# Filler products by an estimated fill, 64-column score products, slack ahead of attention steps, and chunks 8 to 15 in one stretch

## The chip, the cores and the metric

The kernel runs on one core of one Trainium2 chip. The metric is the device time of one execution in microseconds (us), as the median of several runs. The engines are named as in the profile: PE (TensorE, matmuls; PEld is its weight load), DVE (VectorE), ACT (ScalarE), POOL (GpSimd) and SP (SyncE, which issues most DMAs). A line such as L741 is a line of the kernel's file before the change.

## The reference

Eight batches of eight heads, 576 tokens, 64 features a head. For each head two attentions are added: one over q, k and v averaged over groups of four tokens (144 by 144 scores), whose output is repeated four times, and one in a band, where a token sees tokens at a distance under 4. Then the 4608 tokens, 512 features each, go through `h = x @ w_in` (512 to 2048), `g = h * cos(h)` and `g @ w_out` (2048 to 512).

```
scores = where(|i - j| < 4, scale * q @ k.T, -1e9);  out_local = softmax(scores) @ v
out_up = repeat(softmax(scale * mean4(q) @ mean4(k).T) @ mean4(v), 4)
x = (out_up + out_local) laid out as tokens x 512
h = x @ w_in;  out = (h * cos(h)) @ w_out
```

## The kernel before

The FFN works on 12 tiles of 384 tokens and on 16 chunks of 128 of the 2048 hidden features. One **step** is one chunk of one tile: the first product (gemm1, L741, 12 matmuls of 384 columns into a `ph` bank, of which there are two), the activation on ACT and DVE (tr, gh, gl; the DVE operations on tr are L753 and L756, and L756 is the last reader of the `ph` bank), and two steps later on PE the second product (gemm2, L777, 9 matmuls of 512 columns into three `po` banks). Numbers are split into a high and a low part of a shorter format, hence x3h and x3l, gh and gl, wi and wo with two halves. There are 192 steps, counted here from 0; `PASSES` gives their order. The tiles 0, 1 and 2 take turns by four chunks (steps 0 to 47), so that a chunk's weights are needed late; then each tile runs through all 16 chunks (tile 3 is steps 48 to 63, tile 4 steps 64 to 79, and so on). At the end of a pass the `po` banks are copied out (ob, L793) and stored, or added to the output in memory by a DMA that POOL issues (L802). Weights come as 64-bit words and are split on ACT, DVE and POOL (`w_load`, `w_split`, L420 to L431, L399).

The attention works on 32 **units**, a batch and a pair of heads each; a unit has five parts. `u_qk` loads q and k and sums groups of four (qkd, L490); both have one buffer for the batches from 2 on. `u_v` does the same for v. `u_s` computes both scores (from batch 2 on L539, the band, and L555, the averaged tokens), the maxima, the exps and the sums; `u_t` normalizes and transposes (L650) and, from batch 2 on, moves the band's weights by DMA (ptb); `u_pv` multiplies by v (L667 and L686; L679 for the batches 0 and 1) and writes x, from `xd` and `xs` (L698) to x#h (L713) and x#l (L399). The four x tiles form a ring: x3h is the high part of an x tile in place 3. The batches 0 and 1 lie ahead of the steps or between the first ones, with other shapes (L546, L679) and with buffers cut out of weight chunks not loaded yet.

Nothing of the order is written by hand. Every part gives its operations to `Plan.op` with an engine, an estimated duration and its buffers; each has a due time in steps (`at`, `unit`). `Plan.schedule` simulates the engines with priorities and keeps the best of eight rounds; the instructions are then recorded on each engine in the order of the planned starts, and each engine runs its own in order. While recording, wherever PE has a planned hole ahead of 300 us, **wide products** of the identity with itself (L916, 128 by 512, nobody reads them) are put into a free bank for 0.8 of the hole.

## Time and profile before

| what | us |
|---|---|
| median of 3 runs (lowest, highest) | 1006.36 (1006.16, 1006.46) |
| the profiled execution | 1007.08 |
| its span, first to last instruction | 1005.3 |
| PE busy / DVE / ACT / POOL in the span | 985.1 / 678.2 / 610.2 / 223.8 |
| first product of step 0 begins | 52.64 |
| first product of step 4 begins; steps follow without filler from here | 107.18 |
| first product of step 48 begins | 309.84 |

The page gives one profiled execution. Busy time is the time in which an engine computes; an engine that waits for a semaphore, or only issues DMAs, is idle. The granted clock is the share of TensorE's full clock that it was given. A row of the timeline is a group of equal instructions that follow each other: start, time from the first's start to the last's end, what it writes and reads, shapes, count, and in brackets the idle time of the engine ahead of it and what ended it. Matmuls overlap, so the pace of a group is read from its start to the start of the next. A matmul of 32-bit numbers shows as two records.

### The profile page before, as it was taken

The page shows a single profiled execution, that of the slowest core. Times are in us where ns is not written, and L with a number is a line of the kernel's source. Part 1 is how long each engine was busy: PE and PEld are TensorE (multiplying, and loading weights), DVE is VectorE, ACT ScalarE, POOL GpSimd, SP SyncE. Part 2 cuts the span into 40 slices and gives each one's busy share as a digit, 9 for nine tenths or more (in the row PEclk, how much of TensorE's full clock was granted, in tenths as well). Part 3 has the DMA queues.
Part 4 walks back from the last instruction along what each step waited for, and adds up shares of the span by engine and source line. Part 5 has one row for each costly group of instructions (what it writes and reads, how often), then busy time and mean ns, then how long its engine had stood idle before and what let it go on. Part 6 is the DMA issues. An engine that isn't in the chain of part 4 may idle for free.

```text
span 1005.3 us, 23882 instructions
## 1 busy us (share of the span) xinstructions
PE 985.1 (98%) x9932; PEld 850.3 (85%) x9932; DVE 678.2 (67%) x1362; ACT 610.2 (61%) x1174; POOL 223.8 (22%) x280
## 2 busy tenths in 40 slices
PE   8898999999998999999999999999999999999998
PEld 5556898899886888889888888888888888899997
DVE  7699999985686678464758957655657765433433
ACT  4357688876665656555547746654646665655554
POOL 6685334631242203000002211200001300000000
PEclk9699999999999999999999999999999999999999
DMA  7874733332453422210212412201112320100000
GB/s 230 250 249 159 255 119 62 72 59 45 75 131 105 84 66 70 66 33 28 82 48 71 127 49 58 82 26 36 64 52 73 116 60 4 37 1 1 32 1 32
DMA packets 41051, 80.70 MB, mean 80 GB/s; under 512 B 4976, under 2 KB 16240, under 8 KB 40944
## 3 DMA queue, kind: packets, MB, share of 16 engines
q1 hardware_dynamic: 37056, 72.11, 23.2%
q0 software_dynamic: 3888, 7.08, 5.0%
q8 instruction: 78, 1.28, 0.5%
q14 instruction: 29, 0.24, 0.1%
HBM read 57.93 MB, written 16.52 MB: 74 GB/s over the span
## 4 chain that ended last, share of the span: by engine, by line
PE 89%; DVE 5%; DMA 1%; issue 1%; ACT 1%; POOL 1%; SPq 0%; ACTq 0%; POOLq 0%; DVEq 0%
PE bank L777 38%; PE bank L741 38%; PE bank L539 2%; PE bank L916 2%; PE bank L686 2%; PE bank L555 2%; PE bank L667 2%; PE bank L650 1%; DMA q<-qT 1%; PE bank L679 1%; DVE su L610 1%; DVE xxh L421 0%; DVE tr L756 0%; PE bank L546 0%; DVE xxh L425 0%
## 5 line engine op out<-in xcount | busy, mean ns | idle before, releaser
L777 PE MATMUL bank<-wo,gh 128*128 128x512 f32 x1152 | 363.9, 397 | 0.0
L777 PEld LDWEIGHTS bank<-wo,gh 128*128 128x128 f32 x1152 | 210.2, 188 | 38.1 <-issue 3.2
L777 PE MATMUL bank<-wo,gl 128*128 128x512 f32 x576 | 227.7, 396 | 0.0
L752 ACT ACTIVATE tr<-bank,bmagic 128x384 f32<-128x384 f32 x192 | 110.9, 578 | 114.1 <-PE bank L741 109.2
L756 DVE SCALAR_TENSOR_TENSOR tr<-tr,bank 128x384 f32<-128x384 f32 x192 | 105.0, 547 | 108.1 <-ACT tr L751 107.4
L753 DVE SCALAR_TENSOR_TENSOR tr<-tr,bank 128x384 f32<-128x384 f32 x192 | 105.7, 551 | 82.8 <-ACT tr L752 81.8
L750 ACT ACTIVATE tr<-tr 128x384 f32<-128x384 f32 x192 | 100.6, 524 | 77.0 <-DVE tr L753 76.4
L758 ACT ACTIVATE gh<-tr 128x384 fp32r<-128x384 f32 x163 | 85.3, 523 | 91.9 <-DVE tr L756 90.1
L399 DVE TENSOR_TENSOR gl<-tr,gh 128x384 fp32r<-128x384 f32 x154 | 91.7, 596 | 63.5 <-ACT gh L758 59.8
L777 PEld LDWEIGHTS bank<-wo,gl 128*128 128x128 f32 x576 | 108.1, 188 | 23.5
L741 PE MATMUL bank<-x3h,wi 128*128 128x384 f32 x384 | 106.9, 338 | 1.6 <-DVE tr L756 1.0
L741 PE MATMUL bank<-x0h,wi 128*128 128x384 f32 x384 | 107.0, 339 | 0.0
L741 PE MATMUL bank<-x1h,wi 128*128 128x384 f32 x384 | 107.0, 339 | 0.0
L741 PE MATMUL bank<-x2h,wi 128*128 128x384 f32 x384 | 106.8, 339 | 0.0
L751 ACT ACTIVATE tr<-tr 128x384 f32<-128x384 f32 x192 | 100.9, 525 | 6.1
L399 POOL TENSOR_TENSOR gl<-tr,gh 128x384 fp32r<-128x384 f32 x38 | 43.3, 1139 | 268.2 <-DVE gh L759 174.7
L741 PEld LDWEIGHTS bank<-x3h,wi 128*128 128x128 f32 x384 | 70.2, 188 | 4.3 <-DVE tr L756 1.5
L741 PEld LDWEIGHTS bank<-x0h,wi 128*128 128x128 f32 x384 | 70.2, 188 | 2.4 <-DVE wxo L569 0.2
L741 PEld LDWEIGHTS bank<-x1h,wi 128*128 128x128 f32 x384 | 70.2, 188 | 2.4 <-issue 0.4
L741 PEld LDWEIGHTS bank<-x2h,wi 128*128 128x128 f32 x384 | 70.2, 188 | 2.2 <-DVE xxh L425 0.2
L741 PE MATMUL bank<-x3l,wi 128*128 128x384 f32 x192 | 64.6, 336 | 0.1
L741 PE MATMUL bank<-x0l,wi 128*128 128x384 f32 x192 | 64.5, 336 | 0.0
(199 smaller groups left out, 1457.2 us busy)
## 6 DMA issues: line engine op xcount, KB each, us to landing
vl<-vl SPq DMA_DIRECT2D x26, 384.0 KB
out<-ob SPq DMA_DIRECT2D x36, 256.0 KB
wdi<-w_in SPq DMA_DIRECT2D x16, 512.0 KB
wdo<-w_out SPq DMA_DIRECT2D x16, 512.0 KB
q<-qT SPq DMA_DIRECT2D x26, 292.0 KB
k<-kT SPq DMA_DIRECT2D x26, 292.0 KB
vd<-vdn SPq DMA_DIRECT2D x26, 288.0 KB
out<-ob POOLq DMA_DIRECT2D x27, 256.0 KB, 5.3
```

What stands on the lines that cost most here:

```text
L399: f = lambda e: lambda: e.tensor_tensor(out=out(), in0=in0(), in1=in1(), op=ALU.subtract)
L539: pe.matmul(banks[h].get()[BS * g:BS * (g + 1), c:c + BS], q.get()[hs, o:o + BS], k.get()[hs, o:o + BS], start=True, stop=True)
L555: pe.matmul(banks[h].get()[:HD, i * SD:(i + 1) * SD], qkd.get()[hs, 0, i * HD:(i + 1) * HD], qkd.get()[hs, 1, :], start=True, stop=True)
L667: pe.matmul(banks[0].get()[64 * h:64 * h + 64, 2 * SD:3 * SD], vd.get()[:, kh, 64 * h:64 * h + 64], ptd.get()[:, h, kh, :], start=(kh == 0 ...
L741: pe.matmul(ph.get()[:, :m], w[:, i, kc, :], x[:, kc, :], start=(n == 0), stop=(n == 3 * KC - 1))
L750: act.activation(tr.get(), tr.get(), AF.Sin, scale=PI)
L751: return act.activation(tr.get(), tr.get(), AF.Square)
L752: pl.op("ACT", _act(m, True, 1), lambda: act.activation(tr.get(), h(), AF.Identity, bias=bmagic), r=[ph], w=[tr])
L753: pl.op("DVE", _dve(m), lambda: dve.scalar_tensor_tensor(out=tr.get(), in0=tr.get(), scalar=MAGIC, in1=h(), op0=ALU.subtract, op1=ALU.subt ...
L756: pl.op("DVE", _dve(m), lambda: dve.scalar_tensor_tensor(out=tr.get(), in0=tr.get(), scalar=0.5, in1=h(), op0=ALU.subtract, op1=ALU.mult), ...
L758: pl.op("ACT", _act(m, False), lambda: act.activation(gh.get(), tr.get(), AF.Copy), r=[tr], w=[gh], alts=[("DVE", _dve(m / 2), lambda: dve ...
L777: pe.matmul(o, (gh, gh, gl)[k].get()[:, sl], wo.get()[:, (0, 1, 0)[k]], start=(c == c0 and k == 0), stop=(c == c1 - 1 and k == 2))
```

## The change

Three things change, and some with them. (1) While recording, the planner keeps a list of when PE was in use and how far each group fills the array (`util`, its own estimate by shape); ahead of each PE operation planned in its first 115 us, it puts in wide products until its estimated share reaches 0.55. (2) From batch 2 on the band's scores are 24 matmuls of 64 columns instead of 48 of 32: k is loaded into `kz`, which has two planes, one for each head, with zeros in the other head's 64 rows, so that one matmul over all 128 rows gives both heads side by side. Its sums over four tokens are now two DVE instructions, without POOL as the other choice; `ptd` shares its place with `smd`; the band's mask gets 16-bit numbers; in planning, an operation of PE that belongs to these attention parts is assumed ready 0.5 us after an operation of another engine that it needs (`SLACK`); a unit's parts are due 1.1 steps apart instead of 1.4 and units at least 2.25 steps apart instead of 1.5. (3) For tiles 0 to 2, chunks 8 to 15 are one pass instead of two. The core of the diff:

```diff
-PASSES = [(t, c, c + NF) for c in range(0, NC, NF) for t in range(3)] + [(t, 0, NC) for t in range(3, NT)]
+PASSES = [(t, c, e) for c, e in ((0, NF), (NF, 2 * NF), (2 * NF, NC)) for t in range(3)] + [(t, 0, NC) for t in range(3, NT)]
...
+SLACK = 0.5
...
-           fgap=0.4, f0=0.8, fend=300.0, warm=0, fill=0.8)
+           fgap=0.4, f0=0.8, fend=300.0, warm=0, fill=0.8, share=0.55, watch=115.0)
...
+        o.slack = SLACK if eng == "PE" and self.name in ("u_s", "u_t", "u_pv") and self.arg[0] >= NEARLY else 0.0
...
-                    o.preds.append((d, d.lat))
-                    d.succs.append((o, d.lat))
+                    g = d.lat + (0.0 if "PE" in d.alts else o.slack)
+                    o.preds.append((d, g))
+                    d.succs.append((o, g))
...
-    band = const.tile([P, NSEG, BS], F32, name="band")
+    band = const.tile([P, NSEG + 2, BS], BF16, name="band")
+    kz = const.tile([P, 2, SP_], F32, name="kz")
...
-        return sb({"ptl": "sml", "xs": "vd4"}.get(name, name), 2 if name == "ptl" else n, shape)
+        return sb({"ptl": "sml", "xs": "vd4", "ptd": "smd"}.get(name, name), 2 if name == "ptl" else n, shape)
...
+        def load():
+            for hs, h in halves:
+                ins = sp.dma_start(kz[hs, h], kT[b, pr][hs])
+            return ins
+
+        def sums():
+            for hs, h in halves:
+                dve.tensor_reduce(out=qkd.get()[hs, 1], in_=kz[hs, h, PAD:PAD + S].rearrange("p (a r) -> p a r", r=4), axis=AX.X, op=ALU.add)
...
-                for f in range(2):
-                    for n in range(NSEG):
-                        for g in range(4):
-                            h = (g // 2 + f) % 2
-                            hs, o, c = slice(64 * h, 64 * h + 64), (4 * n + g) * BQ, LQ + BS * n
-                            pe.matmul(banks[h].get()[BS * g:BS * (g + 1), c:c + BS],
-                                      q.get()[hs, o:o + BS], k.get()[hs, o:o + BS], start=True, stop=True)
+                for n in range(NSEG):
+                    for g in range(4):
+                        o, c = (4 * n + g) * BQ, LQ + 2 * BS * (n % 3)
+                        pe.matmul(banks[n // 3].get()[BS * g:BS * (g + 1), c:c + 2 * BS].rearrange("p (h n) -> p h n", h=2),
+                                  q.get()[:, o:o + BS], k.get()[:, :, o:o + BS], start=True, stop=True)
...
-            last = max(lo - 2.5 + (hi - lo - 1.0) * i / (NPAIR - 1), last + 1.5)
-            unit(last, 1.4, 2.5, b, i)
+            last = max(lo - 2.5 + (hi - lo - 1.0) * i / (NPAIR - 1), last + 2.25)
+            unit(last, 1.1, 2.5, b, i)
...
+    def wide(s):
+        return pe.matmul(s[2].get(), ident_b, ident_b.unsqueeze(1).broadcast_to([P, 4, P]), start=True, stop=True)
+
+    def share(o, t):
+        e = t + o.dur
+        return (sum(max(0.0, min(y, e) - max(x, e - 3.41)) * u for x, y, u in spent[-60:]) + o.dur * o.util) / 3.41
...
+                    while 4.0 < o.start < CFG["watch"] and share(o, max(cur, o.start)) < CFG["share"]:
+                        wide(s)
+                        spent.append((cur, cur + 0.22, 1.0))
+                        cur += 0.22
```

The planned order then comes out different on every engine. Three places follow, before and changed; in the changed file L563 is the band's scores, L579 the averaged ones, L691 and L710 the value products, L765 and L801 gemm1 and gemm2, L722 the sum that gives xs, L425 to L431 and L403 the weight split and its last part, L924 the wide products.

The first place is on DVE, where the last unit of batch 0 gives its x and chunk 0's weights are split, ahead of step 0. Before:

```order
L698 TENSOR_TENSOR wxo_481<-bank,wxo_396 128x3x96 x2
L423 TENSOR_SCALAR xxh<-xxh 128x512 x2
L425 SCALAR_TENSOR_TENSOR xxh<-wdi_391,xxh 128x512
L425 SCALAR_TENSOR_TENSOR xxh<-wdo_455,xxh 128x512
L698 TENSOR_TENSOR wxi_567<-bank,wxi_559 128x3x96
L427 SCALAR_TENSOR_TENSOR xxh<-wdi_391,xxh 128x512
L427 SCALAR_TENSOR_TENSOR xxh<-wdo_455,xxh 128x512
L698 TENSOR_TENSOR wxi_567<-bank,wxi_559 128x3x96
L399 TENSOR_TENSOR wi_932<-xxh,wi_932 128x512
L399 TENSOR_TENSOR wo_937<-xxh,wo_937 128x512
L399 TENSOR_TENSOR x0l<-wxi_567,x0h 128x384
```

Now:

```order
L722 TENSOR_TENSOR wxo_480<-bank,wxo_396 128x3x96 x2
L658 STREAM_TRANSPOSE wxi_555<-wxi_555 128x384
L429 SCALAR_TENSOR_TENSOR xxh<-wdi_391,xxh 128x512
L427 TENSOR_SCALAR xxh<-xxh 128x512
L431 SCALAR_TENSOR_TENSOR xxh<-wdi_391,xxh 128x512
L429 SCALAR_TENSOR_TENSOR xxh<-wdo_455,xxh 128x512
L722 TENSOR_TENSOR wxi_571<-bank,wxi_555 128x3x96 x2
L431 SCALAR_TENSOR_TENSOR xxh<-wdo_455,xxh 128x512
L403 TENSOR_TENSOR x0l<-wxi_571,x0h 128x384
L403 TENSOR_TENSOR x1l<-wxi_571,x1h 128x192
L403 TENSOR_TENSOR wo_967<-xxh,wo_967 128x512
```

The split of chunk 0 has moved ahead of the last unit's sums (L698 on bank and wxi), and x0l follows those sums almost at once.

The second place is on PE, the start of the unbroken steps (x1h is the x of step 4; the wide products ahead of these rows are left out). Before:

```order
L539 MATMUL bank<-k,q 32x32 x48
L555 MATMUL bank<-qkd 72x144 x4
L741 MATMUL bank<-x1h,wi_932 128x384
L741 MATMUL bank<-x1l,wi_932 128x384
```

Now the scores of the first unit of batch 2 stand behind gemm2 of step 17 and ahead of gemm1 of step 20:

```order
L801 MATMUL bank<-wo_2018,gh 128x512 x2
L801 MATMUL bank<-wo_2018,gl 128x512
L563 MATMUL bank<-kz,q 32x64 x24
L579 MATMUL bank<-qkd 72x144 x4
L765 MATMUL bank<-x2h,wi_1892 128x384
```

They have left the front of the stream and gone into it; wide products fill the place.

The third place is on PE in front of step 64, the first of tile 4, whose x (x0h, x0l) the value products finish. Before:

```order
L667 MATMUL bank<-ptd,vd 64x144 x4
L686 MATMUL bank<-ptb,vl 64x48 x24
L741 MATMUL bank<-x3h,wi_3176 128x384
...
L777 MATMUL bank<-wo_3090,gh 128x512 x2
L777 MATMUL bank<-wo_3090,gl 128x512
L741 MATMUL bank<-x0h,wi_932 128x384
```

Now:

```order
L691 MATMUL bank<-smd,vd 64x144 x4
L710 MATMUL bank<-ptb,vl 64x48 x24
L563 MATMUL bank<-kz,q 32x64 x24
L579 MATMUL bank<-qkd 72x144 x4
L765 MATMUL bank<-x0h,wi_949 128x384
```

Between the value products and the first product that reads their x there was a whole step; now there are only the next unit's scores.

## Rows read from the trace of the kernel before

**Rows 1.** The page: busy time, share and instructions of each engine over the span, then PE's busy share and granted clock in 40 slices of the span, in tenths.

```profile
PE 985.1 (98%) x9932; PEld 850.3 (85%) x9932; DVE 678.2 (67%) x1362; ACT 610.2 (61%) x1174; POOL 223.8 (22%) x280
...
PEclk9699999999999999999999999999999999999999
```

**Rows 2.** The table of stretches: from:to and length in us, busy time and instruction count of each engine in it, granted clock, share of the DMA engines and GB/s.

```profile
23.00:33.00 10.00, 8.96 (x122) 5.62 (x121) 7.53 (x19) 6.19 (x25) 4.63 (x6) 0.50 0.82 249
...
40.00:50.00 10.00, 9.47 (x165) 6.20 (x165) 4.74 (x8) 2.79 (x7) 7.21 (x13) 0.50 0.79 240
50.00:107.00 57.00, 51.06 (x1021) 34.58 (x1019) 55.93 (x109) 37.58 (x97) 38.23 (x42) 1.00 0.64 205
107.00:300.00 193.00, 193.00 (x1517) 172.39 (x1513) 160.04 (x302) 144.07 (x269) 74.64 (x77) 1.00 0.43 98
300.00:321.00 21.00, 17.25 (x220) 13.29 (x220) 13.34 (x31) 10.44 (x18) 6.84 (x10) 0.92 0.45 120
321.00:860.00 539.00, 538.63 (x5462) 474.90 (x5461) 356.67 (x748) 322.96 (x584) 71.58 (x89) 1.00 0.21 61
860.00:1000.00 140.00, 140.00 (x702) 126.49 (x701) 57.33 (x103) 73.98 (x138) 0.00 (x0) 1.00 0.03 12
```

**Rows 3.** The chain of work that ended last, near its end: start, us, what.

```profile
988.56 2.10 PE bank L741 x12
990.66 2.08 PE bank L777 x9
992.75 2.10 PE bank L741 x12
```

**Rows 4.** DVE's timeline ahead of step 0, the three rows with a wait for PE or for a copy behind it (start, us, engine, line, operation, out<-in, shapes, count, idle before).

```profile
30.51 0.31 DVE L466 TENSOR_SCALAR wxi<-bank 128x144 f32<-128x144 f32 x1 [0.85 <-PE bank L667]
...
37.93 0.82 DVE L698 TENSOR_TENSOR wxo<-bank,wxo 128x288 f32<-128x288 f32 x2 [0.86 <-ACT wxo L465]
...
46.65 0.46 DVE L698 TENSOR_TENSOR wxi<-bank,wxi 128x288 f32<-128x288 f32 x1 [5.26 <-ACT wxi L465]
```

**Rows 5.** PE's timeline in the same time.

```profile
25.09 1.05 PE L679 MATMUL bank<-wxi,wxo 32*64 32x24 f32 x28
27.19 2.12 PE L679 MATMUL bank<-wxi,wxo 32*64 32x24 f32 x68 [1.04 <-issue]
...
35.16 0.88 PE L667 MATMUL bank<-wxi 72*64 72x144 f32 x8
35.98 1.59 PE L679 MATMUL bank<-wxo,wxi 32*64 32x24 f32 x96
...
40.13 0.87 PE L546 MATMUL bank<-k,q 64*32 64x32 f32 x48 [1.63 <-issue]
...
41.55 2.33 PE L679 MATMUL bank<-wxi,wxo 32*64 32x24 f32 x76
44.28 0.84 PE L679 MATMUL bank<-wxi,wxo 32*64 32x24 f32 x20 [0.40 <-issue]
45.05 1.23 PE L667 MATMUL bank<-wxo 72*64 72x144 f32 x8
```

**Rows 6.** PE's timeline: 14 wide products at the full clock, and the scores ahead of step 4.

```profile
57.70 3.20 PE L916 MATMUL bank<-ident_b 128*128 128x512 bf16 x14 [0.23 <-ACT smd L597]
...
104.47 0.79 PE L539 MATMUL bank<-k,q 64*32 64x32 f32 x63
```

**Rows 7.** PE's timeline in the steady stretch: a block of scores, a block of value products, eight transposes, each with the row behind it.

```profile
436.05 1.02 PE L539 MATMUL bank<-k,q 64*32 64x32 f32 x96
437.00 0.71 PE L555 MATMUL bank<-qkd 64*72 64x144 f32 x8
...
451.61 0.91 PE L686 MATMUL bank<-ptb,vl 64*64 64x48 f32 x48
452.45 0.50 PE L777 MATMUL bank<-wo,gh 128*128 128x512 f32 x1
...
330.12 0.67 PE L650 MATMUL bank<-ident,smd 72*72 72x72 f32 x8
330.58 0.71 PE L777 MATMUL bank<-wo,gh 128*128 128x512 f32 x2
```

**Rows 8.** PE's timeline around step 48.

```profile
300.39 0.71 PE L667 MATMUL bank<-ptd,vd 72*64 72x144 f32 x8
...
309.84 0.44 PE L741 MATMUL bank<-x3h,wi 128*128 128x384 f32 x1 [1.05 <-DVE tr L756]
...
312.25 0.45 PE L741 MATMUL bank<-x3h,wi 128*128 128x384 f32 x1 [0.56 <-ACT x3h L713]
...
314.24 0.67 PE L650 MATMUL bank<-ident,smd 72*72 72x72 f32 x8 [0.78 <-DVE smd L616]
...
316.33 1.33 PE L539 MATMUL bank<-k,q 64*32 64x32 f32 x92 [0.50 <-ACT ptd L465]
...
320.76 0.33 PE L741 MATMUL bank<-x3h,wi 128*128 128x384 f32 x1
```

**Rows 9.** DVE's timeline ahead of step 48, and the piece of the chain of work in the same time.

```profile
307.05 0.75 DVE L490 TENSOR_REDUCE qkd<-q 128x144 f32<-128x576 f32 x1 [5.31 <-DMA q<-qT]
...
300.30 6.73 DMA q<-qT
```

**Rows 10.** Timelines: value products and the x that follows from them (PE, DVE), the last split of a weight chunk (POOL), the first product of step 39 (PE).

```profile
393.86 0.44 PE L741 MATMUL bank<-x3h,wi 128*128 128x384 f32 x1
...
396.24 0.35 DVE L399 TENSOR_TENSOR x0l<-vd,x0h 128x192 fp32r<-128x192 f32 x1
...
228.07 1.29 POOL L399 TENSOR_TENSOR wo<-xxh,wo 128x512 fp32r<-128x512 f32 x1 [4.89 <-ACT wo L431]
...
258.35 0.33 PE L741 MATMUL bank<-x0h,wi 128*128 128x384 f32 x1
```

**Rows 11.** Groups of instructions by line: count, busy us, mean ns of one, idle before.

```profile
L490 DVE TENSOR_REDUCE qkd<-k 128x144 f32<-128x576 f32 x19 | 14.2, 745 | 1.5 <-DMA k<-kT 1.4
```

More of the change, by code (lines that the diff above doesn't have):

```diff
@@ L75 @@
     __slots__ = ("eng", "dur", "fn", "tab", "deps", "sdeps", "now", "start", "end", "lat", "name", "arg", "preds", "succs",
-                 "i", "fin", "bank", "alts", "boost", "shares")
+                 "i", "fin", "bank", "alts", "boost", "shares", "util", "slack")
 class Plan:
@@ L447, in ub @@
         shape, n, chunk, off = UNIT[name]
+        if name == "k" and (b >= NEARLY or not pr):
+            return pl.buf(lambda: kz if b >= NEARLY else kz[:, 0], "k.0")
         if b == 1 and pr and name in "qk":
@@ L474, in u_qk, with zero @@
         bk = bank(b, "t") if early and ON_PE else None
-        for i, (src, ram) in enumerate(((q, qT), (k, kT))):
+        halves = [(slice(64 * h, 64 * h + 64), h) for h in range(2)]
+        def zero():
+            for hs, h in halves:
+                pool.memset(kz[hs, 1 - h], 0.0)
+        def load():
[3 more added lines that the diff above has]
+        def sums():
+            for hs, h in halves:
+                dve.tensor_reduce(out=qkd.get()[hs, 1], in_=kz[hs, h, PAD:PAD + S].rearrange("p (a r) -> p a r", r=4), axis=AX.X, op=ALU.add)
+        for i, (src, ram) in enumerate(((q, qT), (k, kT))):
+            if i and not early:
+                if b == NEARLY and pr == 0:
+                    pl.op("POOL", 1.5, zero, w=[k])
+                dma(4 * P * SP_, load, pw=[k])
+                pl.op("DVE", 2 * _dve(S), sums, r=[k], pw=[qkd])
+                continue
             dma(4 * P * SP_, lambda src=src, ram=ram: sp.dma_start(src.get(), ram[b, pr]), w=[src])
@@ L915, in attn_ffn_kernel @@
                         for i in range(n):
-                            ins = pe.matmul(s[2].get(), ident_b, ident_b.unsqueeze(1).broadcast_to([P, 4, P]), start=True, stop=True)
+                            ins = wide(s)
+                            spent.append((max(cur, x), max(cur, x) + 0.22, 1.0))
+                            cur = max(cur, x) + 0.22
                             if d and not i:
```

38 lines of the change are left out of this document (20 added, 18 removed).

## The prediction

> **What bounds the kernel now.** I read the page first. TensorE (PE) is busy for 98% of the span, while its granted clock shows one low slice near the start [rows 1]. A busy figure so near the whole cannot say by itself where time is lost, so I went to stretches. By the table of stretches [rows 2] PE computes without a hole from 107 us on, with two exceptions to look at: 300 to 321 us, where 3.75 of 21 us are idle and the clock falls to 0.92 on average, and the time ahead of 107 us, where PE's load is partly filler. In the last stretch, from 860 us, nothing but the two FFN products runs, and the chain shows their pace: 2.10 us for a first product and 2.08 us for a second, so 4.19 us for a step [rows 3]. From 107 us to the end every microsecond of PE work taken away is a microsecond of time; ahead of it, what counts is when the stream can start.
>
> The start belongs to VectorE (DVE): it is busy for 55.93 of the 57 us from 50 to 107 us [rows 2]. But ahead of 50 us it waits. The reader should see three waits in its timeline, 0.85, 0.86 and 5.26 us, each ended by an attention product or by the ACT copy behind one [rows 4]: 6.97 us together. The same stretch on PE shows why the products are late: the clock granted is 0.50 from 23 to 33 us and from 40 to 50 us [rows 2], which is the lower of its two levels (1.2 against 2.4 GHz). There one L679 group, the early value product, takes 1.05 + 2.12 us and another 2.33 + 0.84 us, against 1.59 us at the full clock between them, and L667 takes 1.23 against 0.88 us [rows 5].
>
> **The change, part by part.** *Filler.* There are 24 more wide products, 164 for 140, 8 of them ahead of the first FFN product (75 for 67) and 13 between it and the stream (86 for 73). One takes 3.20/14 = 0.23 us at the full clock [rows 6]. If the clock stays up, the two L679 groups save 1.6 and 1.5 us, the two L667 groups 0.3 to 0.5 us each, the transposes and scores between them about 1 us: some 5 us of PE time, all of it ahead of the 5.26 us wait. DVE can win at most its 6.97 us of waits; nothing, if the clock still falls. I take **5.0 us off**, since one of the small waits also has a load beside it. DVE has the same work ahead of the stream in both orders, 186 and 189 instructions up to the first tr of step 4, so the shift reaches 107 us. The filler's own price runs from nothing to 24 x 0.23 = 5.5 us; PE is idle for 6 of the 57 us from 50 to 107 us [rows 2], which is the cover, so I take **0.5 us on**. Without that cover the 13 there would cost 3 us.
>
> *Score products.* A block of 96 records L539 takes 437.00 - 436.05 = 0.95 us, 9.9 ns for a record of 32 columns [rows 7]. The new block has 48 records of 64 columns, with the two heads side by side. The nearest row is the value product L686: 48 records of 48 columns in 452.45 - 451.61 = 0.84 us, 17.5 ns each, four tiles at a time as here, 64 wide on its stationary side where the new block is 64 wide on its moving side. I take 0.80 us, a little under it because the new stationary side is only 32 wide: 24 x 0.15 = **3.7 us off**. The ends are 48 x 9.9 ns = 0.48 us (11.4 us off), and, were the four tiles of a row group to run one after the other, the pace of a single tile: eight transposes of 72 columns in 0.46 us [rows 7], 0.80 ns a column, 48 x 64 x 0.80 = 2.46 us (36 us on). The Trainium skill's page "TensorEngine Tiling (Array Packing)", section Performance Considerations, says that a matmul carries an overhead of about 60 cycles, so that one of a single column takes as long as one of 60; by that a 64-column product would cost about what a 32-column one does, and the sum would be 7.7 us lower. The rows speak against it here: a record of 48 columns takes 1.8 times what one of 32 does.
>
> *First unit of batch 2.* Its scores stand now at 104.47 us, in front of the stream [rows 6], where DVE is not done with the x of tile 1; filler takes that place in the changed order, and the scores go behind step 19. They cost there 0.95 + 0.64 us: **1.6 us on**, nothing saved if the first product is held by x anyway.
>
> *Slack and spacing.* From 300.39 to 320.76 us PE does two first products and the rest of what 13.3 us hold at the usual pace (2 x 2.10, 2.08, five thirds of 2.08, 0.95, 0.64, 0.64, 0.84, 0.47): 7.1 us lost, of which seams between shapes, common to every unit, are about 0.6 [rows 8]. Cause: DVE, in order, stood 5.31 us on the load of q, which itself took 6.73 us [rows 9], because four units were crowded between steps 41 and 49. Behind that DVE reached neither tr nor x in time, PE stopped, and the clock fell to the lower level. In the changed order the units of batch 2 start behind steps 19, 34, 39 and 43, at least 4 steps, 17 us, apart. I take the whole **6.5 us off** (ends: 0 and 7.1).
>
> But the new order creates three places, in front of steps 48, 64 and 112, where scores stand directly ahead of the first product of a new x tile. At step 64 only 0.80 + 0.64 us lie between the end of the value products and a product that reads their x, and its last quarter needs it 1.6 us later, 3.0 in all; in the trace that x was done 396.59 - 393.86 = 2.7 us behind such products [rows 10]. Then the exps and reductions of the new unit sit ahead of the step's own tr on ACT and DVE, and the product two steps on wants that bank: such a wait is on record with 1.05 us [rows 8]. Three of these: **3.2 us on** (0 to 11).
>
> *One stretch for chunks 8 to 15.* Chunk 15 is first used at step 31, not 39, 8 x 4.19 = 33 us earlier; before, its last split ended at 229.4 us while step 39 began at 258.35 [rows 10]. The changed DVE order has that split's last part behind step 26 (w_in) and 29 (w_out), still 4 to 5 steps ahead of use, 17 us: nothing, unless splits slip by more, and then each microsecond is one. Nine evacuations and nine accumulating stores go: ACT and POOL are not what anyone waits for there, nothing. The reduction of k, 0.74 us each [rows 11], now twice a unit on DVE, adds some 20 us to an engine busy for 357 of 539 us [rows 2]: nothing away from the three places.
>
> **The sum:** -5.0 + 0.5 - 3.7 + 1.6 - 6.5 + 3.2 = -9.9 us. The profiled execution took 1007.08 us (1.8 beyond its span), 0.7 over the median of the runs, so 997.2 there and **996.5 us** as a median. A change under about 2 us, 0.2%, can't be told from none.
>
> **The rivals.**
> 1. *The clock still falls* between 20 and 50 us: the change doesn't do there what it says. For it: the small products and PE's own fetch pauses (1.04 us ahead of 27.19, 1.63 ahead of 40.13 [rows 5]) stay. Against: four more wide products directly ahead of the first value block. Then 996.5 + 5 = 1001.5 us.
> 2. *The score block halves*: records, not columns, set its pace, so half the records take half the time, 0.48 us, and the rest of the sum stays: 988.8 us. For it: the 96 short records now are the fastest on PE; against: L686's pace. This is the case in which the Trainium skill's rule on overhead would hold.
> 3. *The three places cost more.* If each stops PE as the trouble at 309 to 316 us did (idle 1.05, 0.56, 0.78, 0.50 and more, 3.6 us), with one fall of the clock (1.7 us: the 0.92 of the 21 us is 3.4 us at the lower level [rows 2], half of it lost), 10.8 + 1.7 replaces 3.2: 1005.8 us, no change.
> 4. *Slower: the four column tiles of a row group take turns.* Place: every new score block, price up to 1.51 us x 24, so 1036 us. It decides from 0.953 + 6.2/24 = 1.21 us a block, since the rest of the sum is 6.2 us off. Against it: in L539 two column tiles already share a row group, and the pace of 9.9 ns for 32 columns is under half of a single tile's 26.
> 5. *Nothing new waits*, and DVE wins all 7 us: 996.5 - 2 - 3.2 = 991.3 us.
>
> **How the numbers follow.** Forecast 0.45, rivals 0.15, 0.17, 0.12, 0.05, 0.06. The time is the forecast's. The range, 987 to 1005 us, holds all but rival 4 and half of rival 3. Faster by over 0.2% is all of the forecast, rivals 1, 2 and 5, and little of 3: 0.84; within 0.2%: 0.09; slower: 0.07.
>
> **What would show it.** Granted clock 1.0 from 6 us on; no wait of DVE over 1 us ahead of the first FFN product, which comes at 45 to 48 us instead of 52.6, and the stream at 102 instead of 107; the score block at 0.75 to 0.85 us, 1.2 or more being fatal; steps 46 to 51 without holes, PE idle around 1 us each at steps 48 to 50, 64 to 66, 112 to 114. The forecast is wrong if the stream starts no earlier although the clock stays up (then something other than PE's lateness held DVE), or if PE shows waits on weights between steps 28 and 34.

## The result, and the profile after

The changed kernel takes 1011.0 us (median of 12 runs, 1007.2 to 1013.4) against 1005.7 us of the kernel before (12 runs): ratio 1.0062, 95% interval 1.0043 to 1.0082, so 0.6% slower where 1% faster was forecast. The profiled execution took 1011.63 us, its span is 1009.9 us. Three executions on record, two of the experiment b_pass and one of the kernel before, were over 6% longer than the rest of their kernel and are left out of all ratios and counts. Lines have moved: the wide products are L924 (before L916), the score products L563 (L539), the averaged scores L579 (L555), the transposes L674 (L650), the value products L691, L703 and L710 (L667, L679, L686), the first and second FFN product L765 and L801 (L741, L777).

The page (busy time, share and instructions of each engine; PE's granted clock in 40 slices) answers to [rows 1]:

```profile
PE 988.5 (98%) x8804; PEld 841.4 (83%) x8804; DVE 705.2 (70%) x1400; ACT 606.0 (60%) x1176; POOL 184.1 (18%) x233
...
PEclk9899999999999999999999999999999999999999
```

The table of stretches of the changed kernel answers to [rows 2], column for column:

```profile
23.00:33.00 10.00, 9.22 (x229) 5.91 (x228) 8.18 (x22) 7.53 (x30) 5.31 (x8) 0.91 0.77 250
...
40.00:50.00 10.00, 8.62 (x224) 5.63 (x224) 5.62 (x11) 2.45 (x7) 4.02 (x5) 0.75 0.76 232
50.00:107.00 57.00, 53.02 (x919) 34.15 (x917) 55.37 (x110) 36.89 (x95) 35.66 (x41) 0.95 0.66 217
107.00:300.00 193.00, 189.33 (x1288) 165.65 (x1288) 166.11 (x295) 133.49 (x249) 70.24 (x66) 1.00 0.35 83
300.00:321.00 21.00, 20.27 (x201) 16.80 (x201) 15.59 (x35) 10.52 (x21) 1.66 (x3) 1.00 0.29 84
321.00:860.00 539.00, 536.30 (x4596) 468.65 (x4595) 378.64 (x783) 328.49 (x602) 49.21 (x66) 1.00 0.22 63
```

Three things are to be seen. The hole at 300 to 321 us is gone (20.27 us busy, before 17.25). The clock falls less ahead of 50 us (0.91 and 0.75, before 0.50 and 0.50), but a fall stands now in 50 to 107 us too. And PE, which was busy without a hole from 107 to 300 us, has 3.7 us of holes there, and 2.7 us behind 321 us.

Ahead of step 0, DVE's timeline shows waits of 3.79 and 4.38 us (start, us, what, idle before); to be read beside [rows 4]:

```profile
39.37 0.31 DVE L472 TENSOR_SCALAR wxo<-bank 128x144 f32<-128x144 f32 x1 [3.79 <-PE bank L691]
...
48.82 0.82 DVE L722 TENSOR_TENSOR wxi<-bank,wxi 128x288 f32<-128x288 f32 x2 [4.38 <-issue]
```

PE's timeline in front of the second of them, to be read beside [rows 5]:

```profile
42.01 1.20 PE L703 MATMUL bank<-wxi,wxo 32*64 32x24 f32 x63
44.60 0.82 PE L703 MATMUL bank<-wxi,wxo 32*64 32x24 f32 x33 [1.38 <-issue]
45.35 1.89 PE L924 MATMUL bank<-ident_b 128*128 128x512 bf16 x4
47.17 1.23 PE L691 MATMUL bank<-wxo 72*64 72x144 f32 x8
...
52.58 0.53 PE L765 MATMUL bank<-x0h,wi 128*128 128x384 f32 x1
```

The clock is at its lower level here (44.9 to 51.7 us), and four wides of the filler, 0.46 us each, stand between the value products and the L691 behind whose end, at 48.40 us, DVE goes on at 48.82. Step 0 begins at 52.58 us, before at 52.64; step 4, and with it the steady stream, at 108.24 us, before at 107.18.

The new score block, PE's timeline with the row behind it, as [rows 7]:

```profile
440.68 0.88 PE L563 MATMUL bank<-kz,q 128*32 128x64 f32 x48
441.49 0.71 PE L579 MATMUL bank<-qkd 64*72 64x144 f32 x8
```

0.81 us against 0.95, 16.9 ns a record: the forecast size. Where PE waits in the stream (PE's timeline, and one row of DVE's):

```profile
189.84 0.73 PE L801 MATMUL bank<-wo,gh 128*128 128x512 f32 x2 [0.60 <-ACT ob L817]
...
196.24 0.45 PE L765 MATMUL bank<-x0h,wi 128*128 128x384 f32 x1 [0.56 <-DVE tr L780]
...
251.00 1.53 DVE L494 TENSOR_REDUCE qkd<-kz 64x144 f32<-64x576 f32 x2 [2.11 <-DMA kz<-kT]
256.47 0.67 PE L674 MATMUL bank<-ident,smd 72*72 72x72 f32 x8 [0.42 <-DVE smd L640]
258.12 0.45 PE L765 MATMUL bank<-x1h,wi 128*128 128x384 f32 x1 [0.98 <-DVE tr L780]
...
401.21 0.54 PE L563 MATMUL bank<-kz,q 128*32 128x64 f32 x24 [1.15 <-DVE vd L722]
```

DVE, in order, stands 2.11 us on the load of kz, and 5 to 7 us later PE waits for the sums and the tr behind it. Row 401.21 is the tight place at step 64: the second half of the scores needs the bank that DVE is still reading.

The bookkeeping of the stream, from first products in the timelines, for two executions each (the second ones from experiments below that leave the order there as it is; before_look, 1011.99 us, is the longest of the executions of the kernel before that are counted here, so it shows how far an execution can go and not a usual one):

| | step 0 | step 4 | steps 4 to 64 | step 64 to the end |
|---|---|---|---|---|
| before, the profile that was read | 52.64 | 107.18 | 290.96 | 607.2 |
| before, another execution (before_look) | 54.84 | 113.09 | 289.86 | 607.3 |
| changed | 52.58 | 108.24 | 294.09 | 607.5 |
| changed, without 3 wides in the stream (a_fend) | 46.86 | 106.07 | 294.09 | 607.8 |

By place, from the two profiles that were read: the head up to step 4 takes 1.1 us more than before, where the sum had -4.5 (filler and its price); steps 4 to 64 take 3.1 more, where it had about -4.2 (stall -6.5, first unit +1.6, two of the three tight places +2.1, nine score blocks -1.4); the rest takes 0.4 more, where it had about -1.2. Together that is 4.5 us more between these two executions.

### The profile page after: what moved, and what is told of

Read it like the earlier page. It is cut to its first block, busy times and chain, and to the rows that moved or that the text cites. A ratio compares the mean times of both kernels' runs of the same rounds, so it can differ in the third digit from the quotient of the medians.

```text
span 1009.9 us, 21652 instructions
## 1 busy us (share of the span) xinstructions
PE 988.5 (98%) x8804; PEld 841.4 (83%) x8804; DVE 705.2 (70%) x1400; ACT 606.0 (60%) x1176; POOL 184.1 (18%) x233
## 4 chain that ended last, share of the span: by engine, by line
PE 73%; DVE 12%; issue 4%; ACT 3%; DMA 3%; POOL 3%; ACTq 0%; POOLq 0%; DVEq 0%; SPq 0%
PE bank L765 32%; PE bank L801 31%; PE bank L710 2%; PE bank L691 2%; PE bank L924 2%; PE bank L563 2%; DMA vd<-vdn 1%; PE bank L674 1%; PE bank L579 1%; DVE xxh L429 1%; DVE tr L780 1%; DMA q<-qT 1%; DVE su L634 1%; DVE tr L777 1%; DVE qkd L494 1%
## 5 line engine op out<-in xcount | busy, mean ns | idle before, releaser
L801 PE MATMUL bank<-wo,gh 128*128 128x512 f32 x1152 | 362.0, 395 | 0.6 <-ACT ob L817 0.6
L801 PEld LDWEIGHTS bank<-wo,gh 128*128 128x128 f32 x1152 | 211.0, 188 | 39.5 <-issue 2.9
L801 PE MATMUL bank<-wo,gl 128*128 128x512 f32 x576 | 227.8, 396 | 0.0
L777 DVE SCALAR_TENSOR_TENSOR tr<-tr,bank 128x384 f32<-128x384 f32 x192 | 105.1, 547 | 68.4 <-ACT tr L776 67.9
L403 DVE TENSOR_TENSOR gl<-tr,gh 128x384 fp32r<-128x384 f32 x156 | 94.0, 603 | 59.6 <-ACT gh L782 56.1
L782 ACT ACTIVATE gh<-tr 128x384 fp32r<-128x384 f32 x156 | 81.7, 524 | 77.2 <-DVE tr L780 75.7
L801 PEld LDWEIGHTS bank<-wo,gl 128*128 128x128 f32 x576 | 108.0, 188 | 23.6 <-DVE gl L403 0.3
L765 PE MATMUL bank<-x1h,wi 128*128 128x384 f32 x384 | 107.7, 341 | 1.5 <-DVE tr L780 1.5
L765 PE MATMUL bank<-x0h,wi 128*128 128x384 f32 x384 | 107.6, 341 | 1.6 <-DVE tr L780 1.3
L765 PE MATMUL bank<-x2h,wi 128*128 128x384 f32 x384 | 107.7, 341 | 0.3 <-DVE tr L780 0.3
L765 PE MATMUL bank<-x3h,wi 128*128 128x384 f32 x384 | 107.1, 339 | 0.3 <-DVE tr L780 0.3
L403 POOL TENSOR_TENSOR gl<-tr,gh 128x384 fp32r<-128x384 f32 x36 | 41.9, 1164 | 229.3 <-DVE gh L783 132.8
L765 PEld LDWEIGHTS bank<-x0h,wi 128*128 128x128 f32 x384 | 70.2, 188 | 5.7 <-DVE tr L780 3.2
L765 PEld LDWEIGHTS bank<-x1h,wi 128*128 128x128 f32 x384 | 70.2, 188 | 4.7 <-DVE tr L780 2.3
L765 PEld LDWEIGHTS bank<-x2h,wi 128*128 128x128 f32 x384 | 70.2, 188 | 4.2 <-DVE tr L780 2.0
L765 PEld LDWEIGHTS bank<-x3h,wi 128*128 128x128 f32 x384 | 70.2, 188 | 3.7 <-DVE tr L780 1.5
L765 PE MATMUL bank<-x2l,wi 128*128 128x384 f32 x192 | 64.5, 336 | 0.0
L765 PE MATMUL bank<-x1l,wi 128*128 128x384 f32 x192 | 64.5, 336 | 0.0
## 6 DMA issues: line engine op xcount, KB each, us to landing
q<-qT SPq DMA_DIRECT2D x26, 292.0 KB
```

The lines of the kernel that those rows point to most:

```text
L403: f = lambda e: lambda: e.tensor_tensor(out=out(), in0=in0(), in1=in1(), op=ALU.subtract)
L765: pe.matmul(ph.get()[:, :m], w[:, i, kc, :], x[:, kc, :], start=(n == 0), stop=(n == 3 * KC - 1))
L777: pl.op("DVE", _dve(m), lambda: dve.scalar_tensor_tensor(out=tr.get(), in0=tr.get(), scalar=MAGIC, in1=h(), op0=ALU.subtract, op1=ALU.subt ...
L782: pl.op("ACT", _act(m, False), lambda: act.activation(gh.get(), tr.get(), AF.Copy), r=[tr], w=[gh], alts=[("DVE", _dve(m / 2), lambda: dve ...
L801: pe.matmul(o, (gh, gh, gl)[k].get()[:, sl], wo.get()[:, (0, 1, 0)[k]], start=(c == c0 and k == 0), stop=(c == c1 - 1 and k == 2))
```

## The experiments

All ratios are to the kernel before, run beside them on the same chip.

| run | what it is | ratio, 95% interval |
|---|---|---|
| b_fill | before + estimated filling | 0.9996 (0.9978 to 1.0015) |
| b_pass | before + one stretch | 1.0020 (1.0001 to 1.0040) |
| b_fillpass | before + both | 1.0041 (1.0018 to 1.0064) |
| p2 | before + score part with slack and spacing | 1.0040 (1.0012 to 1.0068) |
| p2_noslack | the same, slack 0 | 1.0063 (1.0041 to 1.0086) |
| b_space | before + spacing 2.25 and 1.1 | 1.0070 (1.0049 to 1.0092) |
| b_space225 | before + spacing 2.25 | 1.0072 (1.0049 to 1.0095) |
| a_nofill | changed - filling | 1.0092 (1.0070 to 1.0113) |
| a_pass | changed - one stretch | 1.0108 (1.0084 to 1.0132) |
| a_fend | changed - 3 wides in the stream | 1.0055 (1.0036 to 1.0074) |
| a_07 | changed, slack 0, spacing 1.5 and 0.7 | 1.0002 (0.9984 to 1.0020) |
| b_f50 | before, no wides behind step 0 | 1.0023 (1.0003 to 1.0043) |
| b_vd2 | b_fill, four loads twice | 1.0041 (1.0020 to 1.0062) |
| b_ahead5 | before, 5 loads in flight | 1.0046 (1.0027 to 1.0064) |
| j1 | before, due times 0.05 steps later | 1.0000 (0.9983 to 1.0018) |
| jfill | b_fill with j1 | 0.9987 (0.9972 to 1.0001) |
| jfill_ahead2 | jfill, 2 loads in flight | 1.0122 (1.0099 to 1.0144) |

**Filling and passes, apart.** The changed kernel without the filling, and the kernel before with it alone; the same for the passes.

```diff
 a_nofill:  -share=0.55   +share=0.0
 b_fill:    before + share(), spent, util and the while loop of the diff
 a_pass:    PASSES as before      b_pass: before with the new PASSES
```

> The changed kernel with the share that the filler aims at set from 0.55 to 0: 32 wide products fewer, every engine's other instructions in the same order. Theory A (filler stands in the path): in the changed kernel four wides of 0.46 us each at the lower clock level stand at 45 to 47 us between two attention products, and the DVE waits behind those products came to 9.7 us where they were 7.0; without the wides the stream starts at 105 to 108 us instead of 108.2, and the time is 0 to 3 us under the changed kernel's. Theory B (the filler keeps its promise, something else eats it): the clock falls more (15 us or more at the lower level ahead of 55 us instead of 13.7), the stream starts at 110 us or later, the time is 2 to 5 us above the changed kernel's.

> The kernel before with the estimated filling alone: 26 wide products more, every other instruction in its place. Theory A (filler in the path): the stream starts at 107 to 109 us (before: 107.2), the time is between 0 and 3 us above the kernel before. Theory B (the filling is worth what the prediction had for it, and the new order lost it): the two lower-level stretches ahead of 51 us shorten or go, the DVE wait of 5.26 us halves at least, the stream starts at 102 to 104 us, the time is 3 to 5 us under the kernel before.

> The changed kernel with chunks 8 to 15 of the tiles 0 to 2 in two passes again. Theory A (one stretch brings the weight splits 33 us earlier and crowds DVE): the small waits of PE between 139 and 260 us (0.3, 0.3, 0.9, 0.7, 1.2, 1.8 us over the usual pace, some 5 us) go for the most part, the time is 2 to 5 us under the changed kernel's. Theory B (the stretch costs nothing, as predicted; the waits come from the attention units): the same kind of waits stand there again, the time is within 1.5 us of the changed kernel's.

> The kernel before with chunks 8 to 15 of the tiles 0 to 2 in one pass, nothing else. Theory A (crowding): waits of PE show up between 139 and 260 us, where the kernel before has none, of 2 us or more together; the time is 2 to 4 us above the kernel before, unless the stall of 7 us at 300 to 321 us goes or grows with the new order. Theory B: no waits there, within 1.5 us of the kernel before, with the stall at 300 to 321 us unchanged.

For a_nofill theory B comes nearest: in its profile step 4 stands at 109.67 us, with the clock at its lower level for 36.8 us ahead of it (17.1 in the changed kernel's), and the ratio is 0.30% worse. For b_fill the first half of theory B came and the end is theory A's: in its profile the clock is at its lower level for 6.8 us ahead of the stream, where it was 20.5, and step 0 comes at 48.87 us, 3.8 us earlier. But step 4 comes at 107.78, and the time is that of before. One wait that was not there before stands in POOL's timeline, with PE's first products of the steps 0 and 4 of the same run around it:

```profile
48.87 0.53 PE L741 MATMUL bank<-x0h,wi 128*128 128x384 f32 x1
...
54.65 1.59 POOL L504 TENSOR_TENSOR wxi<-wxi 72x512 f32<-72x512 f32 x1 [4.94 <-DMA wxi<-vdn]
...
107.78 0.44 PE L741 MATMUL bank<-x1h,wi 128*128 128x384 f32 x1
```

POOL, which had not waited there before, waits 4.94 us for the load of v. But that wait is no full answer. jfill, an experiment below, has the same order as b_fill on every engine ahead of step 4, and in its profile POOL waits 0.86 us and step 4 comes at 104.43. Its rows, POOL's and PE's (L900 are the wides there):

```profile
49.76 1.39 POOL L504 TENSOR_TENSOR wxi<-wxi 72x512 f32<-72x512 f32 x1 [0.86 <-DMA wxi<-vdn]
...
98.94 1.25 PE L900 MATMUL bank<-ident_b 128*128 128x512 bf16 x5
100.12 1.59 PE L679 MATMUL bank<-wxi,wxo 32*64 32x24 f32 x96
...
104.43 0.44 PE L741 MATMUL bank<-x1h,wi 128*128 128x384 f32 x1
```

Five wides, 1.18 us, stand here between the last value products ahead of step 4, in b_fill too; in the kernel before nothing stood between these (PE's timeline before):

```profile
101.10 0.71 PE L667 MATMUL bank<-wxo 72*64 72x144 f32 x8
101.74 1.62 PE L679 MATMUL bank<-wxi,wxo 32*64 32x24 f32 x96
```

That is filler in the path, not under cover. How much is to be explained can be estimated from the mean granted clock that is on record for each execution: twice its shortfall from 1, times the span, is the time at the lower level. It is 10 to 36 us, median 22, in 113 executions of the kernel before, and a straight line through them gives 0.27 us of time for each of these us (correlation 0.76). In b_fill's twelve the median is 10 us. By that line the 12 us less are worth about 3.3 us, and the time did not move: the filling did to the clock what it was put there for, and some 3 us went elsewhere, 1.2 of them into these five wides; the rest is open.

In the changed kernel, taking the filling out makes the ratio 0.30% worse, about as much as the interval can tell. The one stretch costs 0.2% alone, at the edge of its interval; but in the changed kernel, with the filling and the score part, the old passes did 0.46% worse than the new (a_pass, whose 18 wides inside the stream took 4.6 us). The waits between 139 and 260 us did go with the old passes, as theory A had it, but the time did not follow. Its profiled execution, at 1011.4 us, was the fastest of six (median 1014.5); what the others lost, and where, is open.

**The score part.** p2 is the changed kernel with `share=0.0` and the old passes; the others:

```diff
 p2_noslack:  p2 with  -SLACK = 0.5   +SLACK = 0.0
 b_space:     before with  -last + 1.5   +last + 2.25   and  -unit(last, 1.4,   +unit(last, 1.1,
 b_space225:  before with  -last + 1.5   +last + 2.25
 b_fillpass:  b_fill with the new PASSES
```

> The score part of the change alone (wide score products, kz, ptd in the place of smd, slack, new spacing), without the estimated filling and with the old passes. Theory A (this part carries the loss): 5 to 8 us above the kernel before; the score block takes 0.81 us, but stream start, small waits and 18 wide products inside the stream eat more than the 3.6 us it saves. Theory B (the parts only hurt each other): within 3 us of the kernel before.

> The score part alone as above, with the slack at 0 instead of 0.5 us. Theory S (the slack is what costs: it makes the planner leave holes, 18 wide products stand inside the stream instead of 8, and PE's instructions are put later than they could go): 4 to 7 us under the run with the slack, 0 to 3 us above the kernel before. Theory K (the wide products' own price: sums of k on DVE alone, one place for ptd and smd, units one behind the other): within 2 us of the run with the slack.

> The kernel before with the new spacing alone (2.25 steps between units, parts 1.1 steps apart), old score products, no slack, no estimated filling, old passes. Theory of the prediction (crowding of the units of batch 2 made the stall at 300 to 321 us): 4 to 7 us under the kernel before. Theory K1 (the serial spacing itself costs, since it pulls the units' parts together): 3 to 6 us above. Theory K2 (spacing is neutral): within 2 us.

> The kernel before with the distance between units raised from 1.5 to 2.25 steps and nothing else (the parts of a unit stay 1.4 steps apart); the first unit of batch 2 starts its scores still behind step 4, the next behind step 24 instead of 20. Theory K1 (the distance itself costs, it moves units to places where PE waits for them): 3 to 7 us above the kernel before, like the run with both changes. Theory K2 (the loss of that run came with the parts 1.1 steps apart): within 2 us.

> The kernel before with the estimated filling and the one pass for chunks 8 to 15, without the score part. If the score part carries the loss (theory A): 0 to 4 us under the kernel before, 6 us or more under the changed kernel. If the loss comes from the parts together (theory B): 2 us or more above the kernel before.

p2, 0.40% above before, lies between its two theories. The spacing alone costs 0.7%, and the distance between units alone as much: K1, and the forecast's theory fell. A different spacing does not remove the wait of DVE for a load, it moves it. In b_space225, DVE's and PE's timelines:

```profile
312.10 0.75 DVE L490 TENSOR_REDUCE qkd<-k 128x144 f32<-128x576 f32 x1 [2.91 <-DMA k<-kT]
...
316.28 0.84 PE L916 MATMUL bank<-ident_b 128*128 128x512 bf16 x2 [2.84 <-DVE su L610]
```

But that is not where most of the 0.7% stands in these two profiles: step 4 comes at 111.07 us in b_space and 110.72 in b_space225, before at 107.18, while steps 4 to 64 take 290.97 and 292.22 us, before 290.96. The spacing of units from batch 2 on also gives DVE, ACT and POOL another order ahead of step 4.

The slack is not the cost in p2: without it the run is no faster (theory K for that run). b_fillpass, 0.4% slower than before, speaks for theory B, loss by the parts together. The measured parts (filling -0.04, one stretch +0.20, score part +0.40%) do make +0.56%, near the 0.62% of the whole, but that is luck, for the pairs do not add up: filling and stretch together cost 0.41% (sum of the parts 0.16), score part and stretch 0.92 (a_nofill; 0.60), score part and filling 1.08 (a_pass; 0.36). Each combination is a new order of the planner with losses of its own, so a part has no price that holds in every combination.

**The planning constants, in the changed kernel.**

```diff
 a_07:  -SLACK = 0.5  +SLACK = 0.0;  -last + 2.25  +last + 1.5;  -unit(last, 1.1,  +unit(last, 0.7,
```

> The changed kernel with the slack at 0, units 1.5 steps apart as before, and a unit's parts 0.7 steps apart; ptd still lies in the place of smd, so a unit's scores still cannot start before the value products of the unit ahead are done, and the scores stand behind almost the same steps as in the changed kernel (44, 48, 52, 56, 60, 65). Theory P (the shared place puts the units one behind the other, and that, not the planning constants, costs): within 2.5 us of the changed kernel, 0.4 to 0.8% above the kernel before. Theory C (slack and spacing cost): within 2 us of the kernel before.

Theory C. With these three numbers the changed kernel is back at the time of before, 6.0 us (0.60%, give or take 0.27) under the change. Which of the three did it was not tested, and the old 1.4 steps between a unit's parts were not tried in the changed kernel. a_07 has a new order too, so it shows what this set of numbers costs against that one; that slack and spacing cost in any order is not shown. PE's order is that of the changed kernel up to and with step 0; its timeline there:

```profile
40.82 0.66 PE L703 MATMUL bank<-wxi,wxo 32*64 32x24 f32 x33 [1.63 <-issue]
41.42 1.04 PE L924 MATMUL bank<-ident_b 128*128 128x512 bf16 x4
42.38 0.71 PE L691 MATMUL bank<-wxo 72*64 72x144 f32 x8
...
45.69 0.52 PE L765 MATMUL bank<-x0h,wi 128*128 128x384 f32 x1
...
102.92 0.44 PE L765 MATMUL bank<-x1h,wi 128*128 128x384 f32 x1
```

In this execution the clock never falls ahead of the stream, and the forecast's times for step 0 and step 4 (45 to 48, 102 us) are there. The four wides take 0.96 us up to the start of the next group, instead of 1.82. The same products in the same order gave 52.58 and 46.86 us in two other executions. In the stream, steps 4 to 64 take 290.0 us, 4.1 less than in the changed kernel, and the rest 609.1, 1.6 more; so of the 7.9 us between the two profiled executions 2.6 are seen in the stream and 5.3 lie ahead of it, where one execution cannot be told from its scatter.

**What holds the start of the stream.**

```diff
 b_f50:         -fend=300.0        +fend=52.0
 b_ahead5:      -AHEAD, FIRST = 3, 40   +AHEAD, FIRST = 5, 40
 jfill_ahead2:  jfill with  AHEAD, FIRST = 2, 40
 b_vd2:         b_fill, the vdn load of batch 1 issued (1 + (b == 1)) times
```

> The kernel before without any wide product behind the first FFN product: 67 of the 140 stay, ahead of it, and 73 go; every other instruction in its place. Theory A (these wides stand in the path of the attention products ahead of the stream): step 4 starts 1 to 4 us earlier than 107.2, the time is 0 to 4 us under the kernel before. Theory B (the filler holds the clock, as the prediction supposed): several stretches at the lower level between 53 and 110 us, step 4 starts 2 to 6 us later, the time is above by as much.

> The kernel before with five instead of three of the first 40 loads in flight, every instruction in its place. Theory L (the loads hold the start: SP issued the v loads of batch 1 and the last weights ahead of step 4 at the same times, whether step 0 started at 52.6 or 48.9 us): the loads between 20 and 60 us come earlier, step 4 starts 2 to 5 us earlier, the time is under the kernel before by as much. Theory D (DVE's and POOL's own work between 50 and 107 us holds it): step 4 within 1 us of 107.2, the time within 1.5 us.

> The kernel before with the estimated filling, and the load of v for each of the four units of batch 1 issued twice (same bytes to the same place, 1.2 MB more between 43 and 60 us); the order of all engines otherwise that of the run with the filling alone. Theory L (the head's loads hold the start of the stream, which is why an earlier first product won nothing): at some 250 GB/s the 1.2 MB take 4.7 us, step 4 starts 3 to 6 us later than 107.8, the time is 3 to 6 us above the run with the filling alone. Theory D (DVE, POOL and PE hold it): less than 1.5 us.

> The kernel before with the estimated filling, the units of batch 2 due 0.05 steps later, and two instead of three of the first 40 loads in flight. Five in flight made the kernel before 0.46% slower; if loads that share the queue with later ones are what comes late (theory L), two in flight make it 0 to 3 us faster than the same kernel with three (0.9987 of before). If the head then runs short of bytes (it moved some 245 GB/s with three), it is 3 to 8 us slower and step 4 starts at 108 us or later.

b_f50: theory B. Without the 73 wides there are four falls of the clock between 53 and 112 us, step 4 stands at 109.07 us, and the kernel is 0.2% slower (0.03 to 0.43); these wides earn their place, if narrowly. b_vd2: theory L. 1.2 MB more load, by estimate 4.7 us at 250 GB/s, cost 4.5 us (0.45% over b_fill, give or take 0.28), and POOL's wait for v is 5.92 us. Step 4 stands at 115.65 us, in an execution 3.6 us over its median, with 17.1 us at the lower clock level between the steps 0 and 4 (b_fill 3.4). So more load there costs time; that less load would win as much is not shown. Nor can the loads be hurried by the number in flight: five move 303 GB/s in 6 to 20 us (three moved 239 in the profile that was read, and 218 to 265 in six other executions), bring the first v load 8 us forward (33.98 us, before 41.82), but the last one is issued at 54.91 us, before at 52.40; step 0 is later (55.19) and so is the stream (112.21). Both theories of that run fell. Two move 172 GB/s there, step 4 slips to 120.28 us, and the kernel is 1.2% slower. Of the three numbers tried, three was best. So the head is sensitive to loads, to PE's products and to the clock.

**What belongs to one execution.**

```diff
 j1:      -last = max(lo - 2.5 +   +last = max(lo - 2.45 +       jfill: the same in b_fill
 a_fend:  -fend=300.0   +fend=112.0       before_look: no edit
```

> The kernel before with the due time of the units from batch 2 on 0.05 steps later (2.45 instead of 2.5 steps ahead), which says nothing about the work: PE's order stays but for 69 rows, DVE's changes around steps 41 to 49. Theory R (the order that the planner finds is a draw, and the one of the kernel before is a good one): 1 to 4 us above or below the kernel before, with other waits between 300 and 340 us. Theory N (small moves in the order mean nothing): within 1 us of the kernel before, with the same stall of 7 us.

> The kernel before with the estimated filling and the units of batch 2 due 0.05 steps later: the two edits that cost nothing, one of which shortened the lower-level stretches and one the stall at 300 to 321 us. If what the profiles showed of them is there in most executions, 2 to 5 us under the kernel before. If it belongs to single executions, within 1.5 us of it.

> The changed kernel without the three ordinary wide products that stand inside its steady stream (213 and 315 us); everything else as it is. Expected if they cost what they take: 0.3 us at 213 us, where PE waits for DVE anyway, 0.66 at 315 us, in all 0.5 to 1 us less, not to be told from none. Rival (they cover a clock fall behind a wait): a fall of the clock shows up in the stream, 1 to 2 us more. The stream's first part, steps 4 to 64, was 294.1 us in the changed kernel's profile and 291.0 in that of before: if this was its own and not that of one execution, it is 292.5 to 294.5 here.

> The kernel before, unchanged, once more: what of its profile is its own. Theory S (the stall at 300 to 321 us is in every execution, and the start of the stream wanders with the clock's falls ahead of it): 6 to 7.5 us lost again between steps 45 and 52, step 4 anywhere from 105 to 111 us. Theory O (the stall belonged to the one execution that was read, which was 2 us slower than most): 4 us or less lost there, step 4 within 1 us of 107.2.

The kernel before, looked at again: step 4 comes at 113.09 us instead of 107.18, with the clock at its lower level for 36.5 us ahead of it, not 20.5; j1, whose order is the same up to there, gives 109.83. By its time j1 speaks for theory N (ratio 1.0000). The stall at 300 to 321 us changes too. DVE's and PE's timelines of before_look, to be read beside [rows 8, 9]:

```profile
310.90 0.75 DVE L490 TENSOR_REDUCE qkd<-q 128x144 f32<-128x576 f32 x1 [3.03 <-DMA q<-qT]
...
317.03 0.44 PE L741 MATMUL bank<-x3l,wi 128*128 128x384 f32 x1 [0.38 <-DVE x3l L399]
318.42 0.66 PE L650 MATMUL bank<-ident,smd 72*72 72x72 f32 x8 [0.77 <-DVE smd L616]
```

DVE's wait for q is 3.03 us, not 5.31, and PE loses 2.6 us there, counted as excess over the usual pace of the groups that exceed it by 0.25 us or more; 3.3 us more go at 336 to 341 us, behind a wait for ptb and with a fall of the clock. The same count at the first place gives 6.8 in the profile that was read, 5.1 in b_f50 and 6.7 in b_ahead5, each with a fall of the clock that begins at 316 to 322 us, and 3.1 in b_fill and 2.3 in b_vd2, without one; all five have the same order there. The stall is in every execution, but its size is not: neither theory S nor theory O. The stream of the changed kernel, by contrast, is its own: 294.09 us for steps 4 to 64 in both executions, with three wides in it and without (a_fend), so these cost nothing that shows. In the kernel before and the four runs with its order there (b_fill, b_vd2, b_f50, b_ahead5) and in before_look it is 287.2 to 292.0 us, so at least 2 us of the loss stand in this stretch whichever execution is taken. jfill has the lowest ratio (1003.59 against 1004.81 us), but its interval takes in 1, as was expected if the shorter stretches and the smaller stall belong to single executions; no version was shown to beat the kernel before.

## Why the prediction was wrong

It failed at two steps of the sum and was too light on others.

- *Slack and spacing, -6.5.* This is the step that failed most. It took the whole stall off and put the constants that were to remove it at no price. The hole at 300 to 321 us did go, but its size was read from one execution; the same order shows 2.3 to 6.8 us there in six. The cause named for it, crowded units, did not lead to the time: spacing them out in the kernel before made it 0.7% slower. And slack and spacing as they were chosen cost about 6 us in the changed kernel (a_07 without them is 0.60% faster). In the changed kernel's stream 0.3 to 1.4 us are lost at each of fifteen places between 139 and 402 us, 9.7 us together by the count used above, where I had looked at three; by that count the kernel before loses 7.5 us from step 4 to step 64 in the profile that was read, a_07 7.3. How much of the 6 us lies ahead of step 4, and by what, is open.
- *Filler, -5.0: "the shift reaches 107 us", since DVE has the same work; and its price, +0.5.* The first half was right: the clock falls less, and step 0 can come at 45.7 to 48.9 us. In the changed kernel's own profile it did not: the clock was at its lower level for 13.7 us ahead of step 0 (20.5 before), four wides at that level stood in front of the products DVE waited for, and step 0 came at 52.58, so rival 1 came in part. The second half failed in b_fill, where 3.8 us at step 0 were gone at step 4; in jfill and a_07 step 4 did come earlier (104.43 and 102.92), but the time of b_fill over twelve executions is 0.04% off before. DVE's equal work was no proof that DVE sets the date: b_vd2 shows that loads do too. And the price was too small: 1.2 us of wides stand in the path in front of step 4 alone. Measured for the term with its price: -0.4 us, +-1.9, where -4.5 stood.
- *Three tight places, +3.2.* Of the right kind and somewhat under: 1.36 us at step 64, 0.66 us (two wides that filled the planned hole) at step 48, none at step 112.
- *One stretch, 0.* It costs 0.2% alone and wins 0.46% (give or take 0.31) in the changed kernel, so no one number replaces the 0. The mechanism named for a cost, splits too late for their steps, did not occur: PE nowhere waits for weights in the stream. DVE is no fuller in b_pass from 107 to 300 us (158.75 us, before 160.04), so what costs the 0.2% is open.
- *Score products, -3.7.* Right: 24 x (0.953 - 0.808) = 3.5 us. The Trainium skill's "TensorEngine Tiling (Array Packing)", Performance Considerations, has one column take as long as 60; an estimate by it would have 64 columns cost about what 32 do. The pace here is 16.9 ns a record against 9.9 ns, but the tiles differ too (128 by 32 against 64 by 32), and so did those of the L686 that the prediction held against the rule (64 by 64); these rows do not test it by itself. And 2.4 us of the gain, what 15 blocks behind step 64 save, came back: 1.3 us in three waits for tr, the rest in small pieces at the changes between groups; from there to the end the changed kernel takes 607.5 us, before 607.2.
- *First unit of batch 2, +1.6.* Right: 0.81 + 0.64 us more in the stream.

Forecast and measured time lie some 16 us apart. By place the two profiles put 5.6 us of the miss ahead of step 4, 7.3 between the steps 4 and 64 and 1.6 behind, 14.5 in all. By part it can't be divided, since the parts do not add up. Of the rivals, 3 had the direction (new waits eat the gain), with a price for three places only; 4, the only one priced on the slower side, was refuted by the block's 0.81 us. That the planner's new order could cost more than the change saves was not among them.

## What to carry to other kernels

A wait read in one execution has a size of that execution: look at a second one before putting the whole of it into a sum, above all where the clock fell in it. A shift gained early in a chain reaches the end only if no other queue (loads, the places they need, another engine) is as late; making that queue later shows whether it counts. And where a planner sets the order, its constants are as much a change as the products are: time them in combination too, since each new order brings its own small waits and the prices of the parts need not add up.

## What the runs showed of the hardware

Identical instruction orders on PE up to step 0 gave step 0 at 45.69, 46.86 and 52.58 us, with the clock at its lower level for 0, 3.4 and 13.7 us ahead of it; four wides in that path took 0.24 us each in the first and 0.46 in the last. Over 113 executions of the kernel before, one us more at the lower level went with 0.27 us more time. The DMA queues moved 172 and 303 GB/s from 6 to 20 us with two and five loads in flight in one execution each, and 218 to 265 with three in seven; the best time was with three.
